# A token assignment that counts with full 128-column weights, in five search steps for six

## The chip, the cores and the metric

The kernel runs on one core of one Trainium2 chip. The metric is the device time of one execution in microseconds (us). TensorE (PE) multiplies, PEld is its loading of the stationary operand (the "weights"), VectorE (DVE), ScalarE (ACT) and GpSimd (POOL) do elementwise work, and SyncE (SP) issues transfers. A lower time is better.

## The reference

Three blocks follow one another: attention with decay, a dense feed-forward layer, and a layer of 8 experts to which tokens are assigned. Only the assignment is touched by the change:

```
logits = x @ w_gate                      # 2304 tokens, 8 experts
cap = N // E                             # 288 places for each expert
for idx in argsort(-logits.flatten()):   # best (token, expert) pair first
    tok, e = idx // E, idx % E
    if assigned[tok] >= 0 or counts[e] >= cap: continue
    assigned[tok] = e; counts[e] += 1
out[mask_e] = relu(x[mask_e] @ w1[e]) @ w2[e]
```

## The kernel before

Attention, then the dense layer's two products, then the experts. The dense layer's second product (`deferred`, products named `acc`) is 864 matmuls of 128 by 128 weights on 512 columns; each group of twelve needs a pair `gh`, `gl`, split on ScalarE (L446) and GpSimd (L447) from what was stored before. Its result goes to `x2d` in HBM through `xo` (L999, L1000), and the experts gather their tokens from there by the indices `ids` (L1082).

The assignment (`routing`) runs at the same time. It works without a sort, in eight phases (`ph`). In each, every unassigned token has one wanted expert (`r_oh`, one-hot over 8) and a key made of its best logit's bits, split into a high half and a low half. The phase looks for the largest threshold at which some expert is wanted by as many tokens as it has free places. All tokens above it are assigned, of those at it as many as there is room for, the full expert is closed, and the next phase begins. The last phase assigns the rest without a search.

The search goes through the two halves of the key (`half`) in three steps each, with 63, 31 and 31 thresholds. One step is:

- VectorE compares 18 x 128 keys with K thresholds, from the base that was found (`r_ge`, L1259).
- TensorE counts for each threshold and expert: 18 products with K columns of `r_ge` as weights and `r_oh` as 8 moving columns, into `q_ct` (L1263, recorded as L1044).
- VectorE compares the counts with the free places (`r_jk`, `r_most`, L1265) and writes which thresholds are reachable (`r_found`, L1266). The three steps' findings lie in three pieces of one column: at rows 0, 64 and 96.
- TensorE adds them up with the step sizes as weights (`r_unit`, 64 + 31 and so on rows), into `q_base` (L1269), which is the next step's base.

Behind a search come two products with a sum over rows (`q_misc` with `r_on` and `r_tru`), the new free places (`r_rp`, `r_r`, `r_nr`), and the head of the next phase: new maximum, new key, the first comparison, and `r_oh`, which is last. I call what stands between `q_misc` with `r_tru` and the next phase's first count a phase head. At the end `q_misc` with `r_tri` numbers the tokens, and a permutation is built (L1337 to L1351): 18 products of 96 weights' columns on 48 columns, which give `ids`.

What sets the order: TensorE's queue is in program order. `routing` is a generator; at each `yield ns` it says how long its chain needs, and the caller puts `acc` products there, 216 ns each, until that time multiplied by a factor is filled (L1049 to L1053). What is left of them comes at the end. The order on VectorE, ScalarE, GpSimd and SP is made by a scheduler, with the tiles' ring buffers as limits. GpSimd also splits weights of the first expert (`wh` L348) as soon as room for them comes free.

Of the kernel before, what the change touches and what calls it, by code (L numbers as in the profile page):

```python
# [46 lines left out]
NA = 2  # L47
# [37 lines left out]
class Plan:  # L85
# [12 lines left out]
    def op(self, eng, ns, fn, needs=(), rank=0.0, takes=(), uses=(), move=0, plain=False, form="A"):  # L98
        o = Op(eng, ns, fn, [x for x in needs if x is not None], rank)
        o.move, o.form = move, form  # L100
        for t in takes:
            if t in self.chained and not plain:
                if self.chained[t] not in (None, o):
                    self.chained[t].followers.append(o)
                    o.left += 1
                self.chained[t] = o
            b = Buffer(t, o)
            o.__dict__.setdefault("got", []).append(b)
        o.uses = list(uses) + list(getattr(o, "got", []))
# [110 lines left out]
def tile_kernel(ctx, tc, q, k, v, f, w_in, w_out, w_gate, w1, w2, out):  # L220
    nc = tc.nc
    w_in, w_out = w_in.bitcast(I32), w_out.bitcast(I32)
    V, A, PE, G = nc.vector, nc.scalar, nc.tensor, nc.gpsimd
# [23 lines left out]
                    compare_op=OP.is_gt, fill=0.0)  # L247
# [257 lines left out]
    with ExitStack() as c1:  # L505
        stp_ = tc.tile_pool(name="sets", bufs=1, side="right", reuse_waits="tile")
        stp = stp_.__enter__()
# [14 lines left out]
        op = plan.op  # L522
# [43 lines left out]
        for i in range(3):  # L566
            n = (i + 1) % 3
# [309 lines left out]
        for g in range(NA + 1):  # L877
# [9 lines left out]
            for j in range(NF if g < NA else 0):  # L887
# [21 lines left out]
                a = op("act", 264, copy, [o], ZV, ["eg"] if j == 0 else (), hb + gb)  # L909
# [13 lines left out]
    with ExitStack() as c1:  # L923
# [5 lines left out]
        op = plan.op  # L929
# [19 lines left out]
        for g in range(NG):  # L949
# [13 lines left out]
            gs, need, bufs = {}, [], []  # L963
# [38 lines left out]
    with ExitStack() as c2:  # L1002
# [4 lines left out]
        with tc.tile_pool(name="ps2", bufs=1, reuse_waits="tile", space=PSUM) as psp, \  # L1007
# [4 lines left out]
            op = plan.op  # L1012
# [35 lines left out]
        rest = deferred(ps, mm)  # L1048
        slack = 0  # L1049
        for ns in routing(nc, rt, ids, ps, W0, mm, vec):  # L1050
            slack += 1.62 * ns
            while slack > 108 and next(rest, None):
                slack -= 216  # L1053
        for _ in rest:
# [3 lines left out]
    with ExitStack() as c3:  # L1058
# [77 lines left out]
        for e in range(E):  # L1136
# [23 lines left out]
def routing(nc, wk, ids, ps, W0, mm, vec):  # L1160
# [26 lines left out]
    steps = []  # L1187
    unit = T("unit", 128, dt=BF)
    found = T("found", 1, dt=BF)
    G.memset(found, 0.0)  # L1190
    on = T("on", 128, dt=BF)
    G.memset(on, 1.0)
    for i, (stp, K) in enumerate(((1024.0, 63), (32.0, 31), (1.0, 31))):
        t = T(f"step{i}", K)
        V.tensor_scalar(t, io[:, 1:K + 1], stp, None, op0=OP.mult)
        G.memset(unit[(0, 64, 96)[i]:], stp)
        steps.append((K, t, (0, 64, 96)[i]))
    we = T("we", E)
    V.tensor_scalar(we, io[:, :E], -1.0, float(E), op0=OP.mult, op1=OP.add)
    eo = T("eo", E)  # L1200
# [16 lines left out]
    nr = T("nr", E)  # L1217
# [10 lines left out]
    for ph in range(E):  # L1228
# [19 lines left out]
        V.tensor_scalar(k2[:, 0], k1, 16, None, op0=OP.logical_shift_right)  # L1248
        V.tensor_scalar(k2[:, 1], k1, 0xffff, None, op0=OP.bitwise_and)
        kf = T("kf", 2, NT)  # L1250
        V.tensor_copy(kf, k2)
        key = kf[:, 0]
        for half in range(2):
            base = None
            for n, (K, kt, at0) in enumerate(steps):
                ct = Q("ct", 512, 2)[:, :E]
                ge = T("ge", NT, 63, dt=BF)
                s = [128, NT, K]
                V.scalar_tensor_tensor(ge[:, :, :K], key[:, :, None].to_broadcast(s), base if n else 0.0,  # L1259
                                       kt[:, None, :].to_broadcast(s), op0=OP.subtract, op1=OP.is_ge)  # L1260
                yield 500 + 19 * K
                for i in range(NT):
                    mm(ct[:K], ge[:, i, :K], oh[:, :, i], start=i == 0, stop=i == NT - 1)  # L1263
                jk, most = T("jk", E), T("most", 1)
                V.tensor_tensor_reduce(out=jk[:K], in0=ct[:K], in1=nr[:K], scale=1.0, scalar=-3e38, op0=OP.add, op1=OP.max, accum_out=most[:K])  # L1265
                V.tensor_scalar(found[at0:at0 + K], most[:K], 0.0, None, op0=OP.is_ge)  # L1266
                base = Q("base", 512)[:, 0:1]
                yield 430
                mm(base, unit[:at0 + K], found[:at0 + K], start=True, stop=True)  # L1269
            yield 480 * (half == 0)  # L1270
            if half == 0:
                k3 = T("k3", NT)
                V.tensor_scalar(k3, key, base, 131072.0, op0=OP.subtract, op1=OP.mult)
# [38 lines left out]
    NA, NB = NTOK // 96, 96  # L1312
# [25 lines left out]
    oa = T("ge", NT, 2, NA, dt=BF)  # L1338
    G.tensor_scalar(oa[:, :, 1], ga, ip[:, 0:1], None, op0=OP.mult)
    V.tensor_tensor(oa[:, :, 0], ga, it[:, :, None].to_broadcast([128, NT, NA]), op=OP.mult)  # L1340
    p = Q("misc", 512)
    for i0 in range(0, NT, 6):
        ob = T("ob", 6, NB, dt=BF, bufs=2)
        s = [128, 6, NB]
        V.tensor_tensor(ob, nb[:, i0:i0 + 6, None].to_broadcast(s), io[:, None, :].to_broadcast(s), op=OP.is_equal)
# [3 lines left out]
    idf = T("idf", NA)  # L1349
# [26 lines left out]
```

## Time and profile before

| | |
|---|---|
| time, median of 3 runs | 977.79 us (976.92 to 982.4) |
| the profiled execution | 976.13 us, span 974.4 us |
| mean granted clock of TensorE | 0.983 |
| busy: PE, PEld, DVE, ACT, POOL | 96%, 83%, 59%, 44%, 45% of the span |
| counts `q_ct`, sums `q_base` | 756 products (42 groups of 18), 42 products |

The span goes from the first to the last instruction. Matmuls are pipelined, so that the recorded length of one (about 0.4 us for an `acc`) is longer than the time to the next one's start; prices on TensorE are therefore read from starts. A row of several is merged, with its count behind x.

### The profile page before, as it was taken

Reading aid. Unit: us, or ns where it says so; the run is one execution under the profiler, and the core shown is the slowest. Engines: PE = TensorE matmul, PEld = TensorE weight load, DVE = VectorE, ACT = ScalarE, POOL = GpSimd, SP = SyncE. Lnnn points to the kernel's source line nnn. Section 1 sums busy time; section 2 is a strip of 40 time slices with the busy share of each in tenths; the row PEclk is TensorE's granted clock in tenths of the full one; section 3 lists DMA queues with packets and bytes.
Section 4 is the critical chain, followed back from the end, with each engine's and each line's share of the span. In section 5 each row is a group of like instructions: output and inputs, shape, how many; then the busy total and the mean of one; then the engine's idle time right before and its main releaser. Section 6 shows DMA issues by size and latency. Waiting matters only on the chain.

```text
span 974.4 us, 21231 instructions
## 1 busy us (share of the span) xinstructions
PE 932.2 (96%) x7923; PEld 805.6 (83%) x7923; DVE 576.5 (59%) x1591; ACT 431.2 (44%) x1077; POOL 440.5 (45%) x568
## 2 busy tenths in 40 slices
PE   6999999999899999999999999999997999999996
PEld 4776778888798998899877777777676999999996
DVE  5788785654578968632535644555563566666641
ACT  5988886776232324422322122222333555555531
POOL 6577783334688848200434443444763112212101
PEclk9999999999899999999999999999997999999998
DMA  5566755533898635531321121121334666557411
GB/s 126 152 179 192 222 160 159 149 122 99 302 368 255 232 124 184 158 86 61 120 65 51 59 65 56 55 65 44 89 128 146 187 193 195 190 191 220 157 60 33
DMA packets 140807, 138.88 MB, mean 143 GB/s; under 512 B 69632, under 2 KB 98816, under 8 KB 140448
## 3 DMA queue, kind: packets, MB, share of 16 engines
q1 hardware_dynamic: 137632, 128.08, 43.2%
q0 software_dynamic: 3072, 9.44, 3.5%
q8 instruction: 62, 1.02, 0.4%
q14 instruction: 41, 0.34, 0.1%
HBM read 106.67 MB, written 30.65 MB: 141 GB/s over the span
## 4 chain that ended last, share of the span: by engine, by line
PE 68%; issue 11%; DVE 10%; DMA 5%; POOL 4%; ACT 1%; SPq 1%; POOLq 0%; DVEq 0%; ACTq 0%
PE acc L1044 20%; PE h L65 18%; PE h L1100 7%; PE y L1113 6%; PE s L65 6%; PE T L65 4%; PE q_ct L1044 3%; DVE kept L65 2%; PE av L65 2%; DMA R<-invd 2%; DVE wbits L65 2%; POOL xt L65 1%; POOL out L1121 1%; DMA X<-xd 1%; SPq L65 1%
## 5 line engine op out<-in xcount | busy, mean ns | idle before, releaser
L65 PE MATMUL h<-X,wh 128*128 128x256 f32 x1728 | 224.4, 286 | 5.7 <-DVE g L65 4.7
L65 PEld LDWEIGHTS h<-X,wh 128*128 128x128 f32 x1728 | 211.3, 191 | 14.0 <-DVE g L65 7.4
L1044 PE MATMUL acc<-wh,gh 128*128 128x512 f32 x576 | 190.4, 404 | 0.0
L447 POOL TENSOR_TENSOR gl<-g,gh 128x512 fp32r<-128x512 f32 x72 | 96.6, 1343 | 111.5 <-ACT gh L446 100.3
L1044 PEld LDWEIGHTS acc<-wh,gh 128*128 128x128 f32 x576 | 109.4, 191 | 20.7
L65 ACT ACTIVATE g<-h 128x256 f32<-128x256 f32 x144 | 55.2, 383 | 156.6 <-PE h L65 153.3
L1044 PE MATMUL acc<-wh,gl 128*128 128x512 f32 x288 | 118.9, 413 | 0.0
L1100 PE MATMUL h<-XE,wh 128*128 128x288 f32 x768 | 118.5, 303 | 0.3 <-ACT XE L1091 0.3
L347 ACT CAST wh<-wst 128x512 fp32r<-128x512 f32 x132 | 79.9, 620 | 82.4 <-DMA wst<-in_moe_w 52.1
L446 ACT CAST gh<-g 128x512 fp32r<-128x512 f32 x72 | 44.5, 621 | 161.8 <-PE acc L1044 131.3
L65 DVE TENSOR_TENSOR wh<-wst,wh 128x512 fp32r<-128x512 f32 x132 | 90.6, 709 | 40.5 <-ACT wh L347 32.0
L1100 PEld LDWEIGHTS h<-XE,wh 128*128 128x128 f32 x768 | 106.6, 191 | 0.6 <-ACT XE L1091 0.6
L65 DVE TENSOR_TENSOR g<-g,h 128x256 f32<-128x256 f32 x144 | 59.9, 416 | 78.3 <-ACT g L65 78.1
L65 ACT ACTIVATE kept<-kept,nm 128x192 f32<-128x192 f32 (+2 forms) x192 | 97.1, 507 | 16.8 <-DVE nm L65 15.7
L1113 PE MATMUL y<-eh,wh 128*128 128x288 f32 x512 | 98.3, 296 | 0.0
L1121 POOL DMA_INDIRECT out<-yo,ids x24 | 24.8, 1034 | 129.2 <-DVE yo L1120 120.0
L1113 PEld LDWEIGHTS y<-eh,wh 128*128 128x128 f32 x512 | 79.5, 188 | 0.2 <-ACT eh L1104 0.2
L65 DVE SCALAR_TENSOR_TENSOR wbits<-w,wbits 128x256 int32<-128x256 int32 x128 | 72.9, 574 | 2.6
L65 DVE CUSTOM_DVE_ANT_0 kept<-s,mask 128x192 f32<-128x192 f32 (+4 forms) x160 | 61.4, 425 | 18.1 <-PE s L65 10.3
L1113 PE MATMUL y<-el,wh 128*128 128x288 f32 x256 | 67.9, 296 | 0.0
L65 ACT ACTIVATE P<-s 128x640 f32<-128x640 f32 (+1 forms) x64 | 53.3, 835 | 26.2 <-PE s L65 24.7
L1044 PEld LDWEIGHTS acc<-wh,gl 128*128 128x128 f32 x288 | 55.1, 191 | 10.9 <-issue 2.0
(197 smaller groups left out, 1613.1 us busy)
## 6 DMA issues: line engine op xcount, KB each, us to landing
wst<-in_moe_w SPq DMA_DIRECT2D x128, 256.0 KB
X<-xd SPq DMA_DIRECT2D x10, 1024.0 KB
gd<-g SPq DMA_DIRECT2D x36, 256.0 KB
g<-gd SPq DMA_DIRECT2D x36, 256.0 KB
w<-in_moe_w_in SPq DMA_DIRECT2D x32, 256.0 KB
w<-in_moe_w_out SPq DMA_DIRECT2D x32, 256.0 KB
xd<-xt SPq DMA_DIRECT2D x16, 320.0 KB
R<-invd SPq DMA_DIRECT2D x32, 144.0 KB
```

What stands on the lines that cost most here:

```text
L65: r = getattr(self.engine, name)(*a, **k)
L347: A.copy(r[u][0], x)
L446: A.copy(gh, g)
L447: G.tensor_tensor(gl, g, gh, op=OP.subtract)
L1044: tc.keep_in_program_order(PE.matmul(*a, **k))
L1100: PE.matmul(h[:, :CAP], w, X[:, c, x, :], start=n == 0, stop=n == 3 * NC - 1)
L1113: PE.matmul(yt[c][:, :CAP], w[:, s], a, start=j == 0 and n == 0, stop=j == NJ - 1 and n == 2)
L1121: sd = G.indirect_dma_start(out=out[:, :], out_offset=bass.IndirectOffsetOnAxis(ap=ids[:, 3 * e + t:3 * e + t + 1], axis=0), in_=y, in_off ...
```

## The change

The search takes 13 bits in the low half and the rest in the high half, instead of 16 and 16. The high half has three steps of 127, 63 and 63 thresholds, the low half two of 127 and 63: 35 steps in seven searched phases, where there were 42. The comparisons of all steps go into one tile `many` with a pitch of 128 or 64 columns for a token group, and each count takes 128 columns of it as weights, whatever lies in those behind the thresholds. The findings are three columns of `found`, already multiplied by the step size, and are added up by products with `rows[K]`, 128 by 128 matrices whose rows from K on are zero: the earlier steps' parts of the sum are issued right behind the counts, the new part where it was. The factor of the filling goes from 1.62 to 1.32. `seg`, the thresholds and some scratch tiles change type or place; the thresholds are made on GpSimd, which also clears `many` once.

```
-            slack += 1.62 * ns
+            slack += 1.32 * ns
...
-    for i, (stp, K) in enumerate(((1024.0, 63), (32.0, 31), (1.0, 31))):
-        t = T(f"step{i}", K)
-        V.tensor_scalar(t, io[:, 1:K + 1], stp, None, op0=OP.mult)
-        G.memset(unit[(0, 64, 96)[i]:], stp)
-        steps.append((K, t, (0, 64, 96)[i]))
+    rows = {}
+    for K in (127, 63):
+        rows[K] = T(f"rows{K}", 128, dt=BF)
+        G.affine_select(rows[K], on, pattern=[[0, 128]], base=K - 1, channel_multiplier=-1, compare_op=OP.is_ge, fill=0.0)
+    steps = []
+    for i, (stp, K) in enumerate(((4096, 127), (64, 127), (1, 63))):
+        t = T(f"step{i}", K, dt=BF)
+        G.iota(t, pattern=[[stp, K]], base=stp, channel_multiplier=0, allow_small_or_imprecise_dtypes=True)
+        steps.append((float(stp), t))
+    halves = [[(127, *steps[0]), (63, *steps[1]), (63, *steps[2])], [(127, *steps[1]), (63, *steps[2])]]
+    many = T("ge", NT * 128, dt=BF)
+    G.memset(many, 0.0)
...
-            for n, (K, kt, at0) in enumerate(steps):
+            for n, (K, stp, kt) in enumerate(kinds):
                 ct = Q("ct", 512, 2)[:, :E]
-                ge = T("ge", NT, 63, dt=BF)
                 s = [128, NT, K]
-                V.scalar_tensor_tensor(ge[:, :, :K], key[:, :, None].to_broadcast(s), base if n else 0.0,
-                                       kt[:, None, :].to_broadcast(s), op0=OP.subtract, op1=OP.is_ge)
+                V.scalar_tensor_tensor(many[:, :NT * (K + 1)].rearrange("p (i k) -> p i k", k=K + 1)[:, :, :K], key[:, :, None].to_broadcast(s), base if n else 0.0,
+                                       kt[:, None, :K].to_broadcast(s), op0=OP.subtract, op1=OP.is_ge)
+                base = Q("base", 512)[:, 0:1]
                 yield 500 + 19 * K
                 for i in range(NT):
-                    mm(ct[:K], ge[:, i, :K], oh[:, :, i], start=i == 0, stop=i == NT - 1)
+                    mm(ct, many[:, (K + 1) * i:(K + 1) * i + 128], oh[:, :, i], start=i == 0, stop=i == NT - 1)
+                for x in range(n):
+                    mm(base, rows[kinds[x][0]], found[:, x:x + 1], start=x == 0, stop=False)
...
-                V.tensor_scalar(found[at0:at0 + K], most[:K], 0.0, None, op0=OP.is_ge)
-                base = Q("base", 512)[:, 0:1]
+                V.tensor_scalar(found[:, n:n + 1], most, 0.0, stp, op0=OP.is_ge, op1=OP.mult)
                 yield 430
-                mm(base, unit[:at0 + K], found[:at0 + K], start=True, stop=True)
+                mm(base, rows[K], found[:, n:n + 1], start=n == 0, stop=True)
...
-    it = T("it", NT)
+    it = T("mw", NT)
```

TensorE, the last search step of the seventh phase, before (`q_ct` counts, `acc` is the dense layer's product, `q_base` the sum):

```order
L1044 MATMUL q_ct<-r_oh,r_ge 31x8
L1044 MATMUL acc<-wh,gh 128x512
L1044 MATMUL acc<-wh,gl 128x512
L1044 MATMUL acc<-wh,gh 128x512
L1044 LDWEIGHTS r_unit
L1044 MATMUL q_base<-r_found,r_unit 128x1
```

and now, the last step of the same phase (`r_rows_7374` has 127 rows of ones, `r_rows_7376` 63):

```order
L1044 MATMUL q_ct<-r_oh,r_ge 128x8
L1044 LDWEIGHTS r_rows_7374
L1044 MATMUL q_base<-r_found,r_rows_7374 128x1
L1044 MATMUL acc<-wh,gh 128x512 x2
L1044 MATMUL acc<-wh,gl 128x512
L1044 LDWEIGHTS r_rows_7376
L1044 MATMUL q_base<-r_found,r_rows_7376 128x1
```

The count's output has 128 rows, and a part of the sum stands directly behind it. In other steps two `acc` products stand where three do here. Between a sum and the next step's count there are 10 or 11 `acc` instead of 8 or 9 (20 or 21 instead of 16 or 17 at the change of half), in a phase head 39 or 40 as before, and ahead of `r_tri` 24 instead of 30. The 18 products of the permutation, which stood behind the last `acc`, now stand as three groups of six with four `acc` between them, and 31 `acc` follow the last.

GpSimd, the end of the stage, before (`r_A` closes the seventh phase, `wh` is the first expert's weights, `r_ge<-r_ga` a part of the permutation, `xe` the first gathers):

```order
L1308 TENSOR_TENSOR r_nr<-r_nr,r_r 128x8
L348 TENSOR_TENSOR wh<-wst,wh 128x512
L1305 TENSOR_TENSOR r_A<-r_A,r_asg 128x144
L447 TENSOR_TENSOR gl<-g_10183,gh 128x512
L1339 TENSOR_SCALAR r_ge<-r_ga,r_ip 128x18x24
L1082 DMA xe<-x2d,ids 96x512 x12
```

and now (`r_mw` is the scratch tile that the token numbers are written into):

```order
L1310 TENSOR_TENSOR r_A<-r_A,r_asg 128x144
L348 TENSOR_TENSOR wh<-wst,wh 128x512
L1338 IOTA r_mw 128x18
L447 TENSOR_TENSOR gl<-g_9934,gh 128x512
L348 TENSOR_TENSOR wh<-wst,wh 128x512
L447 TENSOR_TENSOR gl<-g_9983,gh 128x512
L348 TENSOR_TENSOR wh<-wst,wh 128x512
L1345 TENSOR_SCALAR r_ge<-r_ga,r_ip 128x18x24
L447 TENSOR_TENSOR gl<-g_10017,gh 128x512
L348 TENSOR_TENSOR wh<-wst,wh 128x512
L447 TENSOR_TENSOR gl<-g_10035,gh 128x512
L1082 DMA xe<-x2d,ids 96x512 x12
```

The permutation's step stands among splits of `gl` and `wh` now, which came before it.

## Rows read from the trace of the kernel before

**Rows 1.** Stretches: start:end, length, busy us (instructions) by engine, clock, DMA, GB/s.

```profile
480.00:735.00 255.00, 246.39 (x1695) 183.94 (x1693) 135.16 (x387) 59.92 (x100) 125.88 (x128) 0.98 0.23 68
692.00:696.00 4.00, 4.00 (x27) 2.80 (x26) 0.81 (x1) 1.71 (x3) 1.93 (x2) 0.57 0.21 77
```

**Rows 2.** Timeline of TensorE, third phase: start, length (us), engine, line, operation, shapes.

```profile
546.32 0.18 PE L1044 MATMUL q_misc<-r_rs,r_tru 128*128 128x8 bf16 x1
...
547.13 0.39 PE L1044 MATMUL acc<-wh,gl 128*128 128x512 f32 x1
...
554.84 0.61 PE L1044 MATMUL acc<-wh,gh 128*128 128x512 f32 x2
555.39 0.76 PE L1044 MATMUL q_ct<-r_oh,r_ge 128*63 128x8 bf16 x18
556.07 0.50 PE L1044 MATMUL acc<-wh,gl 128*128 128x512 f32 x1
556.41 0.63 PE L1044 MATMUL acc<-wh,gh 128*128 128x512 f32 x2
...
557.08 0.50 PE L1044 MATMUL acc<-wh,gl 128*128 128x512 f32 x1
...
559.11 0.64 PE L1044 MATMUL q_ct<-r_oh,r_ge 128*31 128x8 bf16 x18
559.68 0.50 PE L1044 MATMUL acc<-wh,gh 128*128 128x512 f32 x1
...
564.16 0.18 PE L1044 MATMUL q_base<-r_found,r_unit 127*128 127x1 bf16 x1
564.20 0.47 PE L1044 MATMUL acc<-wh,gh 128*128 128x512 f32 x1
```

**Rows 3.** Weight loads by shape, 480 to 735: busy us, mean ns; idle time before.

```profile
L1044 PEld LDWEIGHTS <-r_ge 128*31 128x31 bf16 x504 | 15.0, 95 | 10.4 <-issue 9.6 <-DVE r_ge L1259 0.9
L1044 PEld LDWEIGHTS <-r_ge 128*63 128x63 bf16 x252 | 9.4, 113 | 7.0 <-issue 5.4 <-DVE r_ge L1259 1.2 <-DVE r_oh L1238 0.4
L1044 PEld LDWEIGHTS <-r_unit 127*128 127x128 bf16 x14 | 1.4, 98 | 3.8 <-issue 3.8
...
L1044 PEld LDWEIGHTS <-r_ob 128*96 128x96 bf16 x18 | 1.0, 124 | 0.9 <-DVE r_ob L1345 0.7 <-issue 0.2
```

**Rows 4.** Timeline of VectorE, the start of the search and the third phase.

```profile
486.17 0.31 DVE L1238 TENSOR_TENSOR r_oh<-r_mw,r_we 128x144 bf16<-128x144 f32 x1
...
551.77 1.34 DVE L1259 SCALAR_TENSOR_TENSOR r_ge<-r_kf,r_step 128x1134 bf16<-128x1134 f32 x1
553.03 1.40 DVE L1238 TENSOR_TENSOR r_oh<-r_mw,r_we 128x144 bf16<-128x144 f32 x1
...
557.18 0.80 DVE L1259 SCALAR_TENSOR_TENSOR r_ge<-r_kf,q_base,r_step 128x558 bf16<-128x558 f32 x1 [0.55 <-PE q_base L1044]
```

**Rows 5.** Timeline of GpSimd in the same phase head.

```profile
552.84 1.43 POOL L447 TENSOR_TENSOR gl<-g,gh 128x512 fp32r<-128x512 f32 x1 [1.42 <-ACT gh L446]
```

**Rows 6.** Waits of TensorE, 480 to 735: total us, times, longest.

```profile
PE q_ct L1044 <- DVE r_oh L1238: 2.1, 1, 2.1
PE q_misc L1044 <- DVE r_rs L1315: 1.2, 1, 1.2
PE q_misc L1044 <- DVE r_rs L1280: 0.6, 2, 0.3
```

**Rows 7.** Timeline of the stage's end.

```profile
723.99 0.17 PE L1044 MATMUL q_misc<-r_rs,r_tri 128*128 128x8 bf16 x1 [1.20 <-DVE r_rs L1315]
...
726.75 2.40 POOL L1339 TENSOR_SCALAR r_ge<-r_ga,r_ip 128x432 bf16<-128x432 bf16 x1 [4.08 <-DVE r_ga L1337]
...
728.88 0.39 PE L1044 MATMUL acc<-wh,gl 128*128 128x512 f32 x1
...
729.20 0.68 PE L1044 MATMUL q_misc<-r_ge,r_ob 128*96 128x48 bf16 x12
...
732.88 1.17 POOL L1082 DMA_INDIRECT xe<-x2d,ids  x1 [3.73 <-DMA x2d<-xo]
```

More of the change, by code (lines that the diff above doesn't have):

```diff
@@ L1186, in routing @@
     G.iota(io, pattern=[[1, 96]], base=0, channel_multiplier=0, allow_small_or_imprecise_dtypes=True)
[L1187 to L1190, printed above, removed]
+    found = T("found", 3, dt=BF)
     on = T("on", 128, dt=BF)
     G.memset(on, 1.0)
-    for i, (stp, K) in enumerate(((1024.0, 63), (32.0, 31), (1.0, 31))):
-        t = T(f"step{i}", K)
-        V.tensor_scalar(t, io[:, 1:K + 1], stp, None, op0=OP.mult)
-        G.memset(unit[(0, 64, 96)[i]:], stp)
-        steps.append((K, t, (0, 64, 96)[i]))
+    rows = {}
[10 more added lines that the diff above has]
+    G.memset(many, 0.0)
     we = T("we", E)
@@ L1205, in routing @@
     V.tensor_tensor(tru, on, tri, op=OP.subtract)
-    seg = T("seg", E, NT)
+    seg = T("seg", E, NT, dt=BF)
     G.memset(seg, 1.0)
@@ L1247, in routing @@
         k2 = T("k2", 2, NT, dt=I32)
-        V.tensor_scalar(k2[:, 0], k1, 16, None, op0=OP.logical_shift_right)
-        V.tensor_scalar(k2[:, 1], k1, 0xffff, None, op0=OP.bitwise_and)
+        V.tensor_scalar(k2[:, 0], k1, 13, None, op0=OP.logical_shift_right)
+        V.tensor_scalar(k2[:, 1], k1, 0x1fff, None, op0=OP.bitwise_and)
         kf = T("kf", 2, NT)
@@ L1253, in routing @@
         for half in range(2):
-            base = None
-            for n, (K, kt, at0) in enumerate(steps):
+            base, kinds = None, halves[half]
+            for n, (K, stp, kt) in enumerate(kinds):
                 ct = Q("ct", 512, 2)[:, :E]
-                ge = T("ge", NT, 63, dt=BF)
                 s = [128, NT, K]
-                V.scalar_tensor_tensor(ge[:, :, :K], key[:, :, None].to_broadcast(s), base if n else 0.0,
-                                       kt[:, None, :].to_broadcast(s), op0=OP.subtract, op1=OP.is_ge)
+                V.scalar_tensor_tensor(many[:, :NT * (K + 1)].rearrange("p (i k) -> p i k", k=K + 1)[:, :, :K], key[:, :, None].to_broadcast(s), base if n else 0.0,
+                                       kt[:, None, :K].to_broadcast(s), op0=OP.subtract, op1=OP.is_ge)
+                base = Q("base", 512)[:, 0:1]
                 yield 500 + 19 * K
                 for i in range(NT):
-                    mm(ct[:K], ge[:, i, :K], oh[:, :, i], start=i == 0, stop=i == NT - 1)
+                    mm(ct, many[:, (K + 1) * i:(K + 1) * i + 128], oh[:, :, i], start=i == 0, stop=i == NT - 1)
+                for x in range(n):
+                    mm(base, rows[kinds[x][0]], found[:, x:x + 1], start=x == 0, stop=False)
                 jk, most = T("jk", E), T("most", 1)
-                V.tensor_tensor_reduce(out=jk[:K], in0=ct[:K], in1=nr[:K], scale=1.0, scalar=-3e38, op0=OP.add, op1=OP.max, accum_out=most[:K])
-                V.tensor_scalar(found[at0:at0 + K], most[:K], 0.0, None, op0=OP.is_ge)
-                base = Q("base", 512)[:, 0:1]
+                V.tensor_tensor_reduce(out=jk, in0=ct, in1=nr, scale=1.0, scalar=-3e38, op0=OP.add, op1=OP.max, accum_out=most)
+                V.tensor_scalar(found[:, n:n + 1], most, 0.0, stp, op0=OP.is_ge, op1=OP.mult)
                 yield 430
-                mm(base, unit[:at0 + K], found[:at0 + K], start=True, stop=True)
+                mm(base, rows[K], found[:, n:n + 1], start=n == 0, stop=True)
             yield 480 * (half == 0)
@@ L1272, in routing @@
                 k3 = T("k3", NT)
-                V.tensor_scalar(k3, key, base, 131072.0, op0=OP.subtract, op1=OP.mult)
+                V.tensor_scalar(k3, key, base, 16384.0, op0=OP.subtract, op1=OP.mult)
                 V.tensor_tensor(k3, k3, kf[:, 1], op=OP.add)
@@ L1337, in routing @@
     V.tensor_tensor(ga, na[:, :, None].to_broadcast([128, NT, NA]), io[:, None, :NA].to_broadcast([128, NT, NA]), op=OP.is_equal)
-    oa = T("ge", NT, 2, NA, dt=BF)
+    many = T("ge", NT * 128, dt=BF)
+    oa = many[:, :2 * NT * NA].rearrange("p (i a n) -> p i a n", a=2, n=NA)
     G.tensor_scalar(oa[:, :, 1], ga, ip[:, 0:1], None, op0=OP.mult)
@@ L1342, in routing @@
     for i0 in range(0, NT, 6):
-        ob = T("ob", 6, NB, dt=BF, bufs=2)
+        at0 = 2 * NT * NA + i0 % 12 * NB
+        ob = many[:, at0:at0 + 6 * NB].rearrange("p (i n) -> p i n", n=NB)
         s = [128, 6, NB]
-        V.tensor_tensor(ob, nb[:, i0:i0 + 6, None].to_broadcast(s), io[:, None, :].to_broadcast(s), op=OP.is_equal)
+        V.tensor_tensor(ob, nb[:, i0:i0 + 6, None].to_broadcast(s), io[:, None, :NB].to_broadcast(s), op=OP.is_equal)
         yield 600
@@ L1348, in routing @@
             mm(p[:NB, :2 * NA], ob[:, i - i0, :], oa[:, i].rearrange("p a n -> p (a n)"), start=i == 0, stop=i == NT - 1)
-    idf = T("idf", NA)
+    idf = T("kf", NA)
     V.tensor_copy(idf[:NB], p[:NB, NA:2 * NA])
```

## The prediction, made before the changed kernel ran

> **What bounds the kernel now.** I read the busy time by stretch first, to find the stretch that the diff touches: from 480 to 735 us, of 974.4, TensorE is busy 246.4 of 255 us at a mean granted clock of 0.98 [rows 1]. The counting and assignment run there, threaded into 864 products `acc` that use the same engine. Next I read TensorE's timeline, for what an inserted group costs. Between the product at 547.13 and that at 554.84 there are 34 starts in 7.71 us, so an undisturbed product takes 0.227 us [rows 2]. Whatever extends the time between two products beyond that is the price of the routing on TensorE. Then the weight loads by shape [rows 3], VectorE's and GpSimd's rows at one phase head [rows 4, 5], who TensorE waited for [rows 6], and the tail [rows 7]. The stage is bound by TensorE; VectorE's chain ends last only at a few places: TensorE waited 2.1 us once for `r_oh`, 1.2 us once and 0.6 us in two pieces for `r_rs` [rows 6].
>
> The stage's end reaches the run's end through the stores of `x2d`: the last `acc` starts at 728.88, and the first gather is released by the store and starts at 732.88, although the indices are nearly ready by then [rows 7]. So I count time up to the last `acc`, and carry the 4.0 us behind it unchanged. Beyond it, the experts' code is untouched.
>
> **Part 1: what the routing costs TensorE.** A step with 63 thresholds: the product at 554.84 is a pair, so the next would start at 555.29; it starts at 556.07, 0.78 us later, and its own follower only 0.34 us after it, 0.11 more than usual [rows 2]. Price 0.89 us. Of this, 18 pairs of load and product in 0.76 us give (0.76 - 0.18)/17 = 34 ns a pair (0.18 is one product's recorded length); the rest is paid on entering (0.09) and leaving. With 31 thresholds: (0.64 - 0.18)/17 = 27 ns a pair; 0.57 from first count to the next product, with the same 0.09 and 0.11 around it: 0.77 us. The sum that follows (`q_base`) costs 0.22 + 0.11 = 0.33 us where only 63 rows take part (556.41 to 557.08), and 0.04 + 0.11 = 0.15 us with 127 rows (564.16 to 564.20) [rows 2]. I read the difference as the price of going from a full array to a part of it; the new code always takes 128 by 128, or 128 wide.
> Before: 14 x 0.89 + 28 x 0.77 + 14 x 0.33 + 28 x 0.15 = 12.5 + 21.6 + 4.6 + 4.2 = 42.9 us (the loads' counts, 252 and 504, are 14 and 28 groups of 18 [rows 3]).
> After: 35 groups. Entering costs 0.01 and leaving 0.04 + 0.11 as for the full sum, and in between 17 pitches. What is the pitch with 128 columns? Loads of 31, 63 and 96 columns last 95, 113 and 124 ns, but the 128-column ones of `r_unit` 98 [rows 3]: a full load is as short as one of 31. So I take 28 ns. From below the bound is 25 ns, about the 27 of 31 columns; from above 57, if no load is fast: 34 ns at 63 and (0.68 - 0.20)/11 = 44 ns at 96 columns [rows 2, 7], continued to 128. The value follows the single loads, the nearest rows. 0.01 + 17 x 0.028 + 0.15 = 0.64 us, x 35 = 22.4 us. 35 sums at 0.15 = 5.3 us; 28 further sums that stand right behind a group, 0.03 each = 0.8. Three groups of six `q_misc` products now stand ahead of the last `acc` instead of behind it: each 0.09 + 5 x 0.044 + 0.10 + 0.11, together 1.6 us. After: 30.1 us.
> **Saved on TensorE: 12.8 us** (14.6 with 25 ns; a loss of 4.5 with 57).
>
> Here a rule speaks against the change. By the Trainium skill, TensorE: Matmul & The Clock Gate, section LDWEIGHTS (loading the stationary operand), a load takes its number of columns divided by 1.2 in ns, 53 ns at 63 columns; this trace's 34 ns pitch disagrees. Its section Weight-path perf modes (Fast Weight Load) has 128 columns of a type other than fp32 load about twice as fast; both together give an estimate of 53 ns a pair, with which part 1 would lose 2.1 us.
>
> **Part 2: what waits go.** The three waits of 2.1, 1.2 and 0.6 us [rows 6] are tied to the old places, so I take all 3.9 away and price the new places apart. From 692 to 696 the mean clock was 0.57: about 3.4 us at the lower level, behind the 2.1 us wait and a stretch of counts [rows 1, 6]. That lost 1.7 us. Gone: 5.6 us.
>
> **Part 3: what waits come.** The thresholds' comparison on VectorE grows. 1134 elements take 1.34 us, 558 with the base 0.80 [rows 4]; at 0.93 to 1.18 ns an element 2286 elements take 2.4 to 2.7 us, I take 2.5, and 1134 with the base 1.4. Queued behind it are `r_oh`, and TensorE, in order.
> - *Phase heads.* From `q_misc` at 546.32 VectorE needs until 554.43 (end of `r_oh`), TensorE's 39 products until 555.39 [rows 2, 4]. The new comparison adds 1.2 us, the new order leaves 39 or 40 products. In the six such heads VectorE's chain ends 7.2 to 8.7 us after `q_misc`, once 11.2. The spread comes from GpSimd: `r_oh` at 553.03 took 1.40 us and ended with GpSimd's `gl` of 552.84 to 554.27 [rows 4, 5]; the first `r_oh` took 0.31. With 9.0 us of products, new waits of 0.1, 0.4, 1.0, 0, 0, and about 1 in the last: 2.4 us, between 0 and 7.
> - *Inner steps.* Ten products, 2.4 us, cover 0.23 + 1.4 + 0.05 us: no wait, except where GpSimd holds VectorE for another 1.1 us, six in 28 before. 1.0 us. The second half's long comparison has 20 products: covered. Two or three products instead of three or four cover the reduction: just enough, at nothing; without this cover 0.1 us a step, 3.5.
> - *`q_misc` behind the search.* Five or six products instead of seven: 0.9 us, in place of the 0.6.
> - *Start.* GpSimd must clear `r_ge` (2304 wide) and make thresholds before the first comparison, which is itself longer: 0.6 us.
> - *Before `r_tri`.* The chain that took until 723.99, with a wait of 1.2 us behind 30 products, has 24 now, 1.4 us less cover [rows 6, 7]; but the burst of `wh` on GpSimd lies elsewhere. 1.4 us, between 0 and 3.
> - *The permutation.* In the new order of GpSimd, two `gl` and two `wh` stand between the end of phase 8 and `r_ge<-r_ga`, which takes 2.40 us and was free to start before [rows 7]. At about 1.3 us each, this ends some 7.8 us after `r_tri`; TensorE arrives after 22 products, 5.2 us. 2.8 us, between 0 and 4.
> - *`gl` itself.* While `wh` is split, GpSimd needs 2.6 us for each twelve products, which now take 3.1 us, and is held during the longer comparisons. Some `gl` come late: 1.2 us, between 0 and 5.
> - *Clock.* Two waits close together may cost another stretch at the lower level, 1.7 us as above: 1.0.
> Together 11.3 us, between 3 and 21.
>
> **Sum.** -12.8 - 5.6 + 11.3 = -7.1 us. The profiled execution took 976.13 us around its span of 974.4; this gives 969.0. The median shown, 977.79, is 1.7 above it, so I add 1: **970 us**.
>
> **Rivals.**
> 1. *Hardly any new wait.* The fillers are still enough at every place but the permutation: waits of 3.5 us instead of 11.3. For: VectorE's margins at the inner steps were mostly over 1 us. Against: the 2.1 us wait shows one head at its limit already. 962 us.
> 2. *The waits eat the gain.* VectorE and GpSimd block one another longer at each head (1.2 us, six times, as much as the comparison grows), `gl` comes 4 us late, and the clock falls twice: 19 to 20 us of waits. For: 1.40 instead of 0.31 [rows 4]. 978 us: no change.
> 3. *The full load isn't fast in a row; slower than before.* The 98 ns are a single load's latency, and 18 in a row run at the columns' pace, 57 ns: 17 x 35 x 0.029 = +17.3 us, 987 us. It decides from a pitch of 41 ns on ((977.8 - 970)/595 = 13 ns above 28). That would also be the case in which the change doesn't do what it says. Against: the flat 95 to 98 ns. By the two rules of the Trainium skill's page named above the estimate would be 985.
>
> **How the numbers follow.** My forecast (965.5 to 974) 0.46, rival 1 (957 to 965.5) 0.25, rival 2 (974 to 982) 0.20, rival 3 (983 to 991) 0.09. The range from 958 to 981 leaves out rival 3 and the ends of 1 and 2, some 0.18. A measurement of this kernel can tell about 0.5%, 4.9 us: faster is below 972.9, slower above 982.7. Faster: 0.25 + 0.40 = 0.65; same: 0.06 + 0.19 = 0.25; slower: 0.10.
>
> **What would show it.** Part 1: counts of 128 columns at a pitch of 25 to 30 ns, and 0.5 us from first count to next product; 57 ns is rival 3. Part 2: no wait of 2 us at the last head. Part 3: comparisons of 2.4 to 2.7 and 1.4 us, TensorE's waits of about 10 us in all with `r_oh`, `r_rs` and `r_ge` named, the largest ahead of the 96-column products. The last `acc` some 7 us earlier and the first gather 4 us behind it. It would be wrong if the gather were released by the indices, or if the waits lie with `acc`.

## The result and the profile after

The changed kernel takes **968.15 us** (median; 967.2 to 969.65), the kernel before 979.4 beside it: a ratio of 0.9885, 95% interval 0.985 to 0.992. Run once more later, it took 972.41 (971.27 to 975.0) beside 979.93: 0.9925, 0.9897 to 0.9952. So the change brought 1.15% and 0.75%: two measurements of one kernel lie 0.4% apart, with intervals that overlap. The forecast was 970.0, faster.

The profiled execution took 969.65 us, its span is 967.9. The stage is read from the first to the last of the 864 `acc`: 479.57 to 728.88 before, 249.30 us; 481.81 to 721.50 now, 239.69 us, **9.6 less**. Of this the span shows 6.5: the stage began 2.2 us later, behind code that is the same in both, and behind its end TensorE ran longer at the lower clock (724.3 to 738.0, where it was 733.2 to 743.5).

Stretches of the kernel after; columns as in [rows 1]:

```profile
480.00:735.00 255.00, 237.43 (x1626) 183.18 (x1626) 162.88 (x359) 60.98 (x103) 159.37 (x136) 0.97 0.24 74
710.00:715.00 5.00, 4.72 (x28) 3.89 (x29) 1.53 (x2) 1.06 (x2) 4.45 (x4) 0.66 0.15 39
```

Against [rows 1], TensorE is busy 9 us less in these 255, VectorE 28 us more, GpSimd 33 us more, with 136 operations for 128: mostly they are longer, not more. The `gl` splits, 480 to 725, before and then after (busy us, mean ns):

```profile
L447 POOL TENSOR_TENSOR gl<-g,gh 128x512 fp32r<-128x512 f32 x69 | 92.9, 1346 | 111.5 <-ACT gh L446 100.3 <-PE acc L1044 8.3 <-PE q_base L1044 3.0
```

```profile
L447 POOL TENSOR_TENSOR gl<-g,gh 128x512 fp32r<-128x512 f32 x70 | 119.6, 1712 | 70.4 <-ACT gh L446 67.7 <-PE acc L1044 2.5
```

The longer splits lie beside the longer comparisons, and no `acc` waited for them. The second row of stretches holds a stretch at half clock (1.2 GHz). Every kernel here has one at the stage's start (482 to 486 in this one); inside the stage there was one before, behind the 2.1 us wait, and there is one now, behind the longest wait.

Timeline of TensorE, a step with 63 thresholds in the seventh phase, to be laid beside [rows 2]:

```profile
690.92 0.39 PE L1044 MATMUL acc<-wh,gl 128*128 128x512 f32 x1
691.15 0.64 PE L1044 MATMUL q_ct<-r_oh,r_ge 128*128 128x8 bf16 x18
691.64 0.16 PE L1044 MATMUL q_base<-r_found,r_rows 128*128 128x1 bf16 x1
691.66 0.71 PE L1044 MATMUL acc<-wh,gh 128*128 128x512 f32 x2
692.21 0.40 PE L1044 MATMUL acc<-wh,gl 128*128 128x512 f32 x1
692.45 0.18 PE L1044 MATMUL q_base<-r_found,r_rows 128*128 128x1 bf16 x1
```

From the last `acc` to the first count it is 0.23 us, as between two `acc`: the 0.09 that every count with a narrow output paid on entering is gone. 18 counts with 128 columns take 0.64, a pitch of (0.64 - 0.18)/17 = 27 ns, as much as 31 columns had. The weight loads by shape, 480 to 735, beside [rows 3]:

```profile
L1044 PEld LDWEIGHTS <-r_ge 128*128 128x128 bf16 x630 | 19.1, 96 | 13.9 <-issue 9.8 <-DVE r_ge L1262 3.8 <-DVE r_oh L1242 0.3
L1044 PEld LDWEIGHTS <-r_rows 128*128 128x128 bf16 x63 | 5.6, 96 | 9.5 <-issue 9.5
```

Waits of TensorE, 480 to 735 (total us, times, longest), which answer [rows 6]:

```profile
PE q_misc L1044 <- POOL r_ge L1345: 3.0, 1, 3.0
PE q_ct L1044 <- DVE r_oh L1242: 3.0, 3, 2.3
PE q_misc L1044 <- DVE r_rs L1285: 1.3, 2, 1.2
PE q_ct L1044 <- DVE r_ge L1262: 1.1, 1, 1.1
PE q_misc L1044 <- DVE r_rs L1320: 0.3, 1, 0.3
```

8.7 us where there were 3.9. And the end of the stage, for [rows 7]: VectorE's chain from the token numbers to the permutation, GpSimd's part of it, the first of the permutation's products, the last `acc` and the first gather:

```profile
701.83 1.19 DVE L1228 TENSOR_TENSOR_SCAN r_inc<-r_seg,r_A 128x144 f32<-128x144 bf16 x1
...
701.97 0.17 PE L1044 MATMUL q_misc<-r_rs,r_tri 128*128 128x8 bf16 x1 [0.34 <-DVE r_rs L1320]
...
702.67 1.44 POOL L348 TENSOR_TENSOR wh<-wst,wh 128x512 fp32r<-128x512 f32 x1
...
703.11 1.16 DVE L1328 TENSOR_TENSOR r_inc<-r_inc,r_lim 128x144 f32<-128x144 f32 x1
...
704.07 1.35 POOL L447 TENSOR_TENSOR gl<-g,gh 128x512 fp32r<-128x512 f32 x1
...
704.31 1.28 DVE L1329 TENSOR_TENSOR r_inc<-r_inc,r_A 128x144 f32<-128x144 f32 x1
...
706.08 0.70 DVE L1333 TENSOR_SCALAR r_na<-r_df 128x18 f32<-128x18 f32 x1
...
707.12 0.60 DVE L1342 TENSOR_TENSOR r_ga<-r_na,r_io 128x432 bf16<-128x432 f32 x1
...
707.83 2.40 POOL L1345 TENSOR_SCALAR r_ge<-r_ga,r_ip 128x432 bf16<-128x432 bf16 x1 [1.08 <-DVE r_ga L1342]
...
710.28 0.41 PE L1044 MATMUL q_misc<-r_ge 128*96 128x48 bf16 x6 [3.02 <-POOL r_ge L1345]
...
721.50 0.39 PE L1044 MATMUL acc<-wh,gl 128*128 128x512 f32 x1
...
725.51 1.17 POOL L1082 DMA_INDIRECT xe<-x2d,ids  x1 [11.06 <-DMA x2d<-xo]
```

The gather still follows the last `acc` by 4.0 us and is released by the store of `x2d`. The permutation's products wait 3.0 us, and GpSimd itself stood idle for 1.08 us ahead of its step, until VectorE had `r_ga`. The same operations of VectorE in the kernel before, where GpSimd's last split ended at 722.67 and nothing followed it until 726.75:

```profile
723.86 0.45 DVE L1224 TENSOR_TENSOR_SCAN r_inc<-r_seg,r_A 128x144 f32<-128x144 f32 x1
...
724.39 0.31 DVE L1323 TENSOR_TENSOR r_inc<-r_inc,r_lim 128x144 f32<-128x144 f32 x1
724.74 0.31 DVE L1324 TENSOR_TENSOR r_inc<-r_inc,r_A 128x144 f32<-128x144 f32 x1
...
725.53 0.17 DVE L1328 TENSOR_SCALAR r_na<-r_df 128x18 f32<-128x18 f32 x1
...
726.05 0.60 DVE L1337 TENSOR_TENSOR r_ga<-r_na,r_io 128x432 bf16<-128x432 f32 x1
```

There `r_ga` starts 2.06 us behind `r_tri`; now it starts 5.15 us behind it.

### The profile page after: what moved, and what is told of

It reads as the page before. It is cut to its first block, busy times and chain, and to the rows that moved or that the text cites. A ratio compares the mean times of both kernels' runs of the same rounds, so it can differ in the third digit from the quotient of the medians.

```text
span 967.9 us, 20988 instructions
## 1 busy us (share of the span) xinstructions
PE 917.8 (95%) x7818; PEld 800.0 (83%) x7818; DVE 601.2 (62%) x1560; ACT 431.0 (45%) x1077; POOL 466.4 (48%) x570
## 4 chain that ended last, share of the span: by engine, by line
PE 67%; issue 11%; DVE 10%; DMA 5%; POOL 4%; ACT 2%; SPq 0%; POOLq 0%; DVEq 0%; ACTq 0%
PE h L65 19%; PE acc L1044 17%; PE h L1100 7%; PE s L65 7%; PE y L1113 6%; PE T L65 4%; PE av L65 3%; PE q_ct L1044 2%; DVE kept L65 2%; DVE wbits L65 2%; DMA R<-invd 1%; POOL xt L65 1%; POOL out L1121 1%; ACT kept L65 1%; DMA X<-xd 1%
## 5 line engine op out<-in xcount | busy, mean ns | idle before, releaser
L1044 PE MATMUL acc<-wh,gh 128*128 128x512 f32 x576 | 188.4, 403 | 0.0
L447 POOL TENSOR_TENSOR gl<-g,gh 128x512 fp32r<-128x512 f32 x72 | 122.1, 1700 | 70.4 <-ACT gh L446 67.7
L1044 PE MATMUL acc<-wh,gl 128*128 128x512 f32 x288 | 116.2, 404 | 0.0
L1044 PEld LDWEIGHTS acc<-wh,gl 128*128 128x128 f32 x288 | 55.0, 191 | 11.3 <-issue 1.9
```

Of the source, the lines that this page charges most:

```text
L447: G.tensor_tensor(gl, g, gh, op=OP.subtract)
L1044: tc.keep_in_program_order(PE.matmul(*a, **k))
```

## The experiments

Each takes the kernel after, if nothing else is said; "stage" is the time from the first to the last `acc` of the profiled execution. The kernel before, run beside each group of them, took 979.2 to 981.6 us, so times of different groups are compared by their ratio to it.

### Is it the width of the weights, or the number of steps?

**Five steps, but only the thresholds' columns as weights** (the unused rows of `found` cleared once):

```
-                    mm(ct, many[:, (K + 1) * i:(K + 1) * i + 128], ...)
+                    mm(ct[:K], many[:, (K + 1) * i:(K + 1) * i + K], ...)
```

> The changed kernel, but each count takes only its own 127 or 63 columns of the comparison as weights, not 128; the five steps stay. My theory: a load is fast only with all 128 columns. Then the 14 groups of 127 run at a pitch of some 57 ns (34 at 63 and 44 at 96 columns, continued) and cost 0.09 + 17 x 0.057 + 0.21 = 1.27 us instead of 0.6, and the 21 groups of 63 cost 0.89 instead of 0.6: 9 + 6 = 15 us more, 983 us. Rival: what counts is the step from a full array to a part of it, and 127 columns are as good as 128: pitch 27 for them, only the groups of 63 dearer, 6 us more, 974 us. Third: the width does nothing, 968 us.

Measured: 985.67 us (984.64 to 988.81), 1.0055 of the kernel before (1.0036 to 1.0074). The stage takes 258.64 us, 19 more than with full weights. (The sums over counts on VectorE take only the thresholds' rows here as well.) The loads and one count of this kernel:

```profile
L1044 PEld LDWEIGHTS <-r_ge 128*127 128x127 bf16 x252 | 17.2, 140 | 7.5 <-issue 3.9 <-DVE r_ge L1263 2.3
L1044 PEld LDWEIGHTS <-r_ge 128*63 128x63 bf16 x378 | 14.1, 115 | 7.5 <-issue 6.7 <-DVE r_ge L1263 0.7
```

```profile
491.39 1.19 PE L1044 MATMUL q_ct<-r_oh,r_ge 128*127 128x8 bf16 x18 [2.29 <-DVE r_oh L1243]
```

One column less makes a load 140 ns instead of 96, and the pitch (1.19 - 0.18)/17 = 59 ns instead of 27. Without the full width the change would have been a small loss, as the theory had it.

**Six steps as before, with 128 columns** (the kernel before, its comparison written with a pitch of K + 1 into a wide tile, which GpSimd clears once):

```
-                    mm(ct[:K], ge[:, i, :K], oh[:, :, i], ...)
+                    mm(ct, wide[:, (K + 1) * i:(K + 1) * i + 128], oh[:, :, i], ...)
```

> The kernel before with its six steps, its sums and its filling, but with counts of 128 columns at a pitch of 64 or 32. Theory: the width alone brings 42 groups from 0.89 (14) and 0.77 (28) down to about 0.6 us, 8.9 us less, and up to 1 us is lost to waits at the phase heads, where less time is covered: 971 us against 979. Rival: the gain came from having fewer steps and sums: then no more than 2 us faster, 977 or more.

Measured: 969.86 us (964.74 to 975.91), 0.9891 (0.9835 to 0.9946); the stage takes 238.25 us, 11.0 less than before and no more than after the whole change. Its loads and waits:

```profile
L1044 PEld LDWEIGHTS <-r_ge 128*128 128x128 bf16 x756 | 22.6, 96 | 13.8 <-issue 9.7 <-DVE r_oh L1240 2.8 <-DVE r_ge L1260 1.2
```

```profile
PE q_ct L1044 <- DVE r_oh L1240: 2.1, 1, 2.1
PE q_misc L1044 <- DVE r_rs L1316: 1.2, 1, 1.2
PE q_misc L1044 <- DVE r_rs L1281: 0.6, 2, 0.3
```

The waits of [rows 6], unchanged. The width alone brings the gain; the larger, fewer steps bring nothing on top that these runs could tell.

**Does the place of the weights matter?** A pitch of K + 2 instead of K + 1, so that the weights start at odd columns too.

> The changed kernel with token groups at a pitch of 129 and 65 columns instead of 128 and 64, so that every second count's weights start at an odd column, two bytes off a word. If the start matters, half of the 630 loads go at the slow pitch of about 57 ns: 595 x 0.030 / 2 = 9 us more, 977 us, and two pitches in the trace. If it doesn't, one pitch of 27 ns and 968 us. By the Trainium skill, TensorE: Matmul & The Clock Gate, section Weight-path perf modes, a fast load reads 32 bits at a time, and among its conditions none is on the start; that would leave the time as it is.

Measured, in one run: 970.6 us, stage 239.24:

```profile
L1044 PEld LDWEIGHTS <-r_ge 128*128 128x128 bf16 x630 | 19.3, 97 | 12.5 <-issue 10.3 <-DVE r_ge L1262 1.9 <-DVE r_oh L1242 0.3
```

97 ns, and a pitch of 27 again. The aligned strides are not needed; the 128 columns are.

### What is the smaller factor worth?

The factor of the filling back to 1.62:

```
-            slack += 1.32 * ns
+            slack += 1.62 * ns
```

> The changed kernel with the old filling factor, 1.62 instead of 1.32. Each phase head has 48 products instead of 39, so the waits for the one-hot of wanted experts at the heads (0.7 us without the first) and for the long comparison (1.1 us) go. But the 864 products are used up before the seventh phase is done, and the rest of the chain lies open: about 1.2 phases of 28 us with 12 us of products missing in each. Theory: 10 to 20 us slower, 978 to 988 us, with TensorE's waits at the end of the stage. Rival: the factor doesn't matter, within 3 us of 968.

Measured, in one run: 978.21 us, the lower end of what was expected. The last `acc` starts at 706.63 already, but the first gathered tile is transposed at 737.88, 31 us behind it instead of 7.5: the `acc` run out before the routing ends, and its last phase stands open.

```profile
PE q_ct L1044 <- DVE r_ge L1262: 7.6, 4, 3.1
```

Ahead of the permutation it waits 5.0 us, ahead of `r_tri` 4.1. TensorE ran at the lower clock from 712 to 746 there.

### Why does TensorE wait ahead of the permutation?

**GpSimd's step given to VectorE:**

```
-    G.tensor_scalar(oa[:, :, 1], ga, ip[:, 0:1], None, op0=OP.mult)
+    V.tensor_scalar(oa[:, :, 1], ga, ip[:, 0:1], None, op0=OP.mult)
```

> The changed kernel, with one difference: the permutation's step that fills the second half of its 48 columns (r_ge from r_ga and the row number, 2.40 us on GpSimd in the profile after) is done by VectorE. It tells apart why TensorE waited 3.0 us ahead of the permutation. Theory of the prediction: GpSimd's queue is the cause (splits of gl and wh ahead of that step). Then VectorE, which is free there, ends the step earlier, and the 3.0 us wait falls to under 1 us; the stage gets 2 to 3 us shorter, about 966 us. Rival, from the profile after: r_ga itself is late (5.15 us behind r_tri, where it was 2.06 before), since the small operations of VectorE ahead of it each last 0.7 to 1.3 us beside GpSimd's; GpSimd idled 1.08 us for it. Then the step only moves to an engine that is held at that place anyway, and TensorE still waits 2 us or more; the time stays at 967 to 970.

Measured, in one run: 974.28 us, stage 247.13, longer than either side expected. The wait got longer, not shorter:

```profile
PE q_misc L1044 <- DVE r_ge L1346: 4.7, 1, 4.7
```

The step itself takes only 0.32 us on VectorE, where it took 2.40. But with GpSimd free for two more splits at that place, two more of VectorE's small operations lasted 1.19 us instead of 0.18, and the chain ended later. The queue of GpSimd, which the prediction named, is not the cause; the rival holds. (The time itself says little: of the 7.4 us by which this stage is longer, some 6.8 are lost at half clock. From 490 to 498 the mean clock is 0.57, from 674 to 679 it is 0.66 and from 711 to 720 it is 0.62, where the kernel after has only its 0.66 from 710 to 715.)

**The weights' splits taken off GpSimd** (the low parts of the first expert's weights, `wh`):

```
-            lo_on = G if e == 0 else vec
+            lo_on = V if e == 0 else vec
```

> The changed kernel, with the low parts of the first expert's weights (wh, 16 operations of 1.3 to 1.4 us on GpSimd) made by VectorE. It asks whether GpSimd's splits are what stretches VectorE's chain ahead of the permutation. There, in the profile after, four small operations took 1.19, 1.16, 1.28 and 0.70 us beside an unbroken row of gl and wh splits, where the same four took 0.45, 0.31, 0.31 and 0.17 in the kernel before, with GpSimd idle: 3.09 us more, which is all by which r_ga was later behind r_tri (5.15 and 2.06 us). Theory: with every second split gone from GpSimd, at most two of the four are still held; r_ga comes 2.5 to 4 us behind r_tri and the wait of 3.0 us falls to between 0 and 1.5. The two waits of 1.1 and 1.2 us in the seventh phase may go too. Time 965 to 967. Rival: the operations are long for another reason (the scan and the 144-wide tiles of the new layout), or the splits on VectorE delay the chain as much: the wait stays at 2.5 us or more, and the time at 968 to 972.

Measured: **964.95 us** (962.64 to 966.8), 0.9847 (0.9823 to 0.9871), beside 972.41 for the kernel after on the same chip; the ranges do not touch. Stage 234.51 us, 5.2 less than in the first profile of the kernel after: the waits listed there came to 8.7 us and come to 5.1 here, and the stretch at half clock behind the permutation, 1.7 us, is gone (mean clock 1.00 from 700 to 715). VectorE's chain in this kernel:

```profile
698.31 0.45 DVE L1228 TENSOR_TENSOR_SCAN r_inc<-r_seg,r_A 128x144 f32<-128x144 bf16 x1
...
698.84 0.31 DVE L1328 TENSOR_TENSOR r_inc<-r_inc,r_lim 128x144 f32<-128x144 f32 x1
699.18 1.36 DVE L1329 TENSOR_TENSOR r_inc<-r_inc,r_A 128x144 f32<-128x144 f32 x1
...
701.54 0.60 DVE L1342 TENSOR_TENSOR r_ga<-r_na,r_io 128x432 bf16<-128x432 f32 x1
```

The same scan, on the same tiles, takes 0.45 instead of 1.19 us; only the one operation that met the remaining `gl` split (699.09 to 700.38) is still long. `r_ga` comes 3.1 us behind `r_tri`, not 5.15, and the largest of the waits are (the others add 1.1)

```profile
PE q_ct L1044 <- DVE r_oh L1242: 1.5, 3, 0.8
PE q_misc L1044 <- DVE r_ge L1346: 1.3, 1, 1.3
PE q_misc L1044 <- DVE r_rs L1320: 1.2, 1, 1.2
```

3.0 became 1.3 ahead of the permutation, and the start's 2.3 us went too: two of the splits stood there, and without them GpSimd clears the wide tile at 480.42, 0.2 us behind the first `acc`, where it was 2.4 us behind it. Ahead of `r_tri` 0.3 became 1.2, because one split now stands in VectorE's own chain. By the Trainium skill, SBUF — State Buffer, section Who interferes with whom, a VectorE operation with two inputs in SBUF contends with a GpSimd operation that reads SBUF; the trace agrees for the scan and the two `r_inc`, which took 0.74 to 0.97 us longer beside the splits. The fourth, `r_na`, has one input tile and took 0.53 longer.

### Can the waits be covered?

**More `acc` ahead of the permutation** (`yield 3000` to `yield 5200` behind `r_tri`: 36 instead of 22).

> The changed kernel, with 36 instead of 22 acc products ahead of the permutation (the one chain length given there goes from 3000 to 5200 ns); fewer are left behind it. Theory: the wait of 3.0 us and the stretch at half clock of about 3.4 us behind it (1.7 us lost) are both there only because 22 products, 5.0 us, don't cover the chain from r_tri to the permutation, about 8 us. With 36 (8.2 us) the wait goes to under 0.5 us, the half-clock stretch ahead of the stage's end goes with it, and the stage is 3 to 4.7 us shorter: 963.5 to 965 beside 968 for the changed kernel. Rival: the indices then come later, and the first gather is released by them instead of by the store of x2d: then as much is lost behind the last acc as is won ahead of it, the distance from the last acc to the first gather transpose grows from 7.5 us by 2 us or more, and the time stays at 967 to 969.

**The wide tile cleared by VectorE** (`V.memset(many, 0.0)`).

> The changed kernel, with the one clearing of the wide tile (2304 columns, 2.0 us on GpSimd in the profile after) done by VectorE. Theory: the first count waited 2.3 us, because VectorE's first steps of the search lasted 3.2 and 1.3 us while GpSimd worked without a break (weights, thresholds, clearing), and the clearing is the largest part that the change added there. With it on VectorE, which is idle earlier, the wait is 0.3 us or less and the time about 966. Rival: VectorE is held by the other GpSimd work there just as long (splits of wh and the thresholds are still in a row): the wait stays over 1.5 us and the time at 968.

**Both.**

> The changed kernel with both edits: 36 products ahead of the permutation, and the clearing on VectorE. If the waits at the start (2.3 us) and at the permutation (3.0 us, with 1.7 us of half clock behind it) add up as separate places, the gains add up too: 968 - 2 - 4 = 962 us, 0.6% under the changed kernel. If a wait that is removed at the start comes back at a later place of the same chain (the acc products are a fixed stock, and 14 more of them stand late now), it stays at 965 to 966.

Measured on one chip, without the kernel after: 968.94 us (967.79 to 971.07), 970.12 (967.78 to 971.29) and **965.66** (963.89 to 967.13); of the kernel before 0.9879 (0.9848 to 0.9909), 0.9884 (0.9852 to 0.9915), 0.9844 (0.9821 to 0.9867). Each wait went where it was to go: no wait is left ahead of the permutation in the first, none at the start in the second. What held VectorE at the start is seen in one operation, in the kernel after and, beside it, GpSimd's clearing:

```profile
483.48 3.23 DVE L1249 TENSOR_SCALAR r_k<-r_m 128x18 int32<-128x18 int32 x1
...
484.19 2.02 POOL L1201 MEMSET r_ge<- 128x2304 bf16 x1
```

and with the clearing on VectorE:

```profile
483.17 0.38 DVE L1249 TENSOR_SCALAR r_k<-r_m 128x18 int32<-128x18 int32 x1
```

Yet neither edit alone brought the 2 to 4 us of time that had been expected of it. Their stages took 240.29 and 241.19 us, since stretches at the lower clock in other places took the gain: 490 to 498 in the first has a mean clock of 0.57, behind the same wait of 2.3 us at the start behind which the kernel after keeps its clock of 1.00:

```profile
490.00:498.00 8.00, 6.97 (x51) 5.05 (x51) 2.71 (x7) 0.62 (x1) 2.86 (x2) 0.57 0.22 59
```

```profile
493.00:500.00 7.00, 6.54 (x62) 5.03 (x62) 3.79 (x11) 1.24 (x2) 3.19 (x3) 1.00 0.28 73
```

In both, a wait of 1.9 us for `r_oh` at the seventh head was followed by another such stretch. The two edits together had neither: stage 232.65 us, 7.0 less than the kernel after, with no stretch at the lower clock but the one at its start. Expected were 962 us, and 965 to 966 if a wait came back later. No wait did, and 7.0 us is what the start's 2.3, the permutation's 3.0 and the 1.7 of half clock behind it add up to. But 1.4 us of it are lost behind the last `acc`, and the kernel before took 981.63 us beside these runs, 2.2 more than beside the first result, so that 965.66 doesn't speak for the rival. The rival of the first experiment is there in part. With fewer `acc` behind the permutation the last four stores of `x2d` bunch. With both edits the third copy into `xo` waits for a buffer that a store still holds,

```profile
711.45 1.27 ACT L999 COPY xo<-acc 128x512 f32<-128x512 f32 x2 [4.07 <-PE acc L1044]
715.54 1.22 ACT L999 COPY xo<-acc 128x512 f32<-128x512 f32 x2 [2.82 <-DMA x2d<-xo]
```

so that the first gathered tile comes 8.8 us behind the last `acc`, not 7.5. It is not the indices that come late, as the rival had it: they were there at 711.1.

**Three edits together** (the splits and the clearing on VectorE, 3800 for 3000), with the kernel after once more beside it.

> The changed kernel once more, to stand beside the next two on the same chip: 968 to 970 us, waits of TensorE as in the first profile after (3.0 us ahead of the permutation, 2.3 us at the start). The stretches at the lower clock inside the stage may lie elsewhere.

> The changed kernel with three edits: the wide tile cleared by VectorE, the first expert's weights' low parts made by VectorE, and a chain length of 3800 instead of 3000 ns ahead of the permutation (some five acc more there). If the three places are separate, the start's wait (2.3 us), the permutation's (3.0 us) and the half-clock stretch behind it (1.7 us) all go, with enough acc left behind it for the stores of x2d not to bunch: 968 - 6 = 962 us, with an undisturbed 7.5 us from the last acc to the first gather transpose. If VectorE becomes the late one in the seventh phase, where half of its splits now stand, new waits for r_oh or r_ge of 1 to 2 us each take their place and it stays at 965 or above.

Measured: the kernel after 972.41 us, where 968 to 970 were expected, stage 242.48; in this execution it had a wait of 1.9 us at the seventh head in place of the 1.1 for the long comparison, and 1.7 us more at half clock behind the permutation. With the three edits 965.59 (963.13 to 968.02), 0.9856 (0.983 to 0.9882): no better than the splits alone. The stage took 236.02 us, 1.5 more than theirs, and it has a stretch of 3 us at half clock, from 671 on, that the other did not have.

### Do fewer steps pay once VectorE is free?

The six-step kernel with 128 columns, and `lo_on = V` as above.

> The kernel before with 128-column counts (six steps) and the first expert's weights' low parts made by VectorE. It asks whether five search steps pay against six once GpSimd's splits no longer hold VectorE. Counted: from first to last acc the six-step kernel took 238.25 us with GpSimd's splits, the five-step one with VectorE's 234.5. Theory: in the six-step order the waits were 2.1 us at the seventh head, 1.2 ahead of r_tri, 0.6 and 0.6; VectorE's splits take away about 1 us of the 2.1 and add as much elsewhere; the stage stays at 236 to 238 us, 966 to 969 us in all, 0.985 to 0.989 of the kernel before, so that the fewer steps are worth 2 to 3 us there. Rival: five steps give nothing here either: the stage falls to 234.5 as well, 965 us, 0.984 to 0.985.

Measured: **964.33 us** (963.17 to 966.64), 0.9841 (0.9811 to 0.987), stage 234.79 us. The rival holds: six steps and five end alike, 234.79 and 234.51. The six-step kernel's waits, all that lie in the stage:

```profile
PE q_misc L1044 <- DVE r_rs L1281: 0.6, 2, 0.3
...
PE q_misc L1044 <- DVE r_rs L1316: 0.2, 1, 0.2
```

0.8 us against 5.1 with five steps. What seven steps fewer save on TensorE (some 5 us, read from the starts), the longer comparisons give back in waits. Three kernels come out at 0.984 to 0.985 of the kernel before (this one, the five steps with the splits on VectorE, and the two edits that cover the waits), where the changed kernel has 0.989 and 0.993; these runs can't tell which of the three is best.

## Why the prediction was right, point by point

- **What bounds the stage, and its end: right.** TensorE's row of `acc` sets the time, 4.0 us lie between the last of them and the first gather as in [rows 7], and the time followed the stage.
- **Part 1, the price on TensorE: right in kind, too small in size.** The pitch is 27 ns (28 taken, bounds 25 and 57). 35 groups with the products behind them cost 21.0 us, not 23.2: from the starts, a group adds 0.58 to 0.63 with these products, where 0.64 and 0.03 for each product were counted. The 35 sums cost 0.14 each, 4.9 instead of 5.3. What the permutation's groups cost can't be told from the wait ahead of them; in the two kernels without that wait three groups cost 1.0, where 1.6 were counted. Together that is 26.9 us. The old groups and sums, read in the same way, cost 42.2, so that some 15.3 us are saved instead of 12.8. Taking the single full load of [rows 3] as the nearest row was the choice that decided; rival 3, which needed 41 ns, is refuted by 27. In the kernel with narrow weights 127 columns have a pitch of 59 ns. By the Trainium skill, TensorE: Matmul & The Clock Gate, section Weight-path perf modes — Fast Weight Load (FWL) and DoubleRow, the fast load comes at 128 columns of a type other than fp32, and about halves the time: the trace agrees, 59 against 27. Columns divided by 1.2, 106 ns by its section LDWEIGHTS (loading the stationary operand), is not what 127 columns took here, so that the estimate from both, 985, missed.
- **Part 2, 5.6 us gone: as said**, 3.9 of waits at the old places and 1.7 for the half-clock stretch at 692.
- **Part 3, 11.3 us of waits come: the sum is right (11.6), its parts are not.** The six heads were to cost 2.4 and cost 0.7; `gl` 1.2 and 0; ahead of `r_tri` 1.4 and 0.3. The start was to cost 0.6 and cost 2.3, since the length of GpSimd's clearing was counted, but not that VectorE would be held all along it. The long comparison of the second half was called covered; in the seventh phase, beside GpSimd's weight splits, it took 3.58 us and TensorE waited 1.1. Behind the search it is 1.3 for 0.9, the inner steps' short waits come to about 1.2 (read from starts) for 1.0, the permutation 3.0 for 2.8, the clock 1.7 for 1.0. Misses of both signs cancelled, so that the sum came out by luck. (For the permutation, its own 7.8 and 5.2 leave 2.6, not 2.8; 22 products at 0.227 are 5.0.) In the second run of the same kernel the seventh head alone had 1.9 us: these parts are not stable to a microsecond.
- **The mechanism at the permutation: the place and the price right, the cause not.** It was to be GpSimd's queue. It is VectorE: four of its operations took 3.09 us longer beside the splits than in the kernel before (1.19, 1.16, 1.28, 0.70 against 0.45, 0.31, 0.31, 0.17), which is the whole delay of `r_ga`; giving GpSimd's step away made the wait longer, giving its splits away shortened it.
- **What the prediction did not ask:** it priced width and fewer steps as one saving. By its own prices, six steps with full weights save 42.9 - (42 x 0.64 + 14 x 0.33 + 28 x 0.15) = 7.2 us, and with the 0.58 that a group took 9.7, without any of the new waits. The width alone gave 11.0, of which 1.7 is the half-clock stretch that was gone. The steps' share is saved on TensorE and lost again in waits.
- **Sum:** -15.3 - 5.6 + 11.6 = -9.3 us, where the stage shows -9.6; the span shows 6.5 of it.

## What to carry to other kernels

Price a small group inside a full TensorE queue by the starts around it, and look whether a full 128-column operand costs less than a narrow one: here columns that nobody reads made it cheaper. A step that saves work on the bound engine by giving a helper engine longer operations is worth only what the cover left on that chain allows; price the two apart. And when a chain of small VectorE operations is late, look at what GpSimd does beside it before its own queue.

## What was not expected of the hardware

- Counts with 127 columns of weights run at a pitch of 59 ns, those with 128 at 27, as fast as with 31; odd starting columns make no difference (97 against 96 ns a load).
- A VectorE operation on 18 elements lasted 3.23 us, 483.48 to 486.71, beside short GpSimd operations and a clearing of 2.02 us that followed one another without a gap; without the clearing among them it lasted 0.38.
- The same wait of 2.3 us at the same place was followed by 6.9 us at the lower level (1.2 GHz) in one kernel and by none in another. A wait of 1.9 us at the seventh head was followed by 3.4 us at that level in the two kernels with one edit each, and by none when the kernel after ran again (mean clock 1.00 from 673 to 678). What decides it stays open. Such a stretch moves the stage by 1.7 or 3.4 us, as much as the waits themselves.
